# One VectorE instruction fewer per piece of float64 weights, and a new table of costs for the planner, in a fused attention and two-MoE kernel

## The chip, the cores and the metric

One core of one Trainium2 chip runs the whole kernel as one program. The metric is device microseconds of one execution; lower is better. TensorE is called PE here, VectorE DVE, ScalarE ACT, GpSimd POOL, and SP is the engine that issues almost all transfers.

## The reference, cut to what matters

```python
# q, k, v: 4 batches, 8 heads, 576 rows, 64 wide
scores = scale * (q @ k.T)
kth    = the 32nd largest score of each row
attn   = softmax(scores where scores >= kth else -1e9) @ v
x  = attn laid out as [2304, 512]
x2 = ((x @ w_a) * (x @ w_b)) @ w_out      # w_a, w_b 512 x 1536, w_out 1536 x 512, all float64
# second part: 8 experts, each token goes to the expert with the largest logit
logits = x2 @ w_gate
out[token] = gate_w[token] * (relu(x2[token] @ w1[e]) @ w2[e])
```

`w_a`, `w_b` and `w_out` arrive as float64, and no engine computes in float64: the kernel makes float32 of them by handling the two 32-bit words of each number.

## The kernel before, in words

**Weights.** `conv` (L367 to L392) turns one piece of 128 x 512 float64 numbers into float32. There are 36 pieces: 24 of `w_a` and `w_b`, 12 of `w_out`. For one piece SP loads the words (L371); ACT takes the absolute value of the high word with its exponent rescaled (L383); DVE shifts it left by three places and clears the sign (L385); ACT makes the sign, +1 or -1, of the high word (L387); DVE shifts the low word right by 29 and ORs its three top bits in (L388); POOL multiplies by the sign (L391). `split` then cuts the float32 number into a high part (ACT, L396) and a rest (POOL, L397), and both parts are stored in DRAM, in `ws` (L412) for `w_a` and `w_b` and in `wos` (L420) for `w_out`. The pieces use six buffers that belong to later stages (`gT1`, `gH1`, `xh1`, `xl1`, `gT0`, `gH0`), so the traces name them by those.

**Attention.** There are 144 tiles of 128 rows. For a pair of tiles PE makes scores `sp` (L521, or L502 for a tile of leftover rows), ACT copies half of them to `s` (L527), DVE takes the maximum `m` and the minimum `n` of the two halves (L535), and then finds the 32nd largest value with rounds of MAX8 and MATCH_REPLACE8 (L546 to L573). POOL scales the row maximum to `nm` (L549), ACT makes the exponentials `e` (L554), DVE masks and sums them to `am` (L601), PE transposes `am` to `tp` (L627, L609), ACT copies it to `aT` (L631), and PE multiplies by v (L648). `attn_norm` multiplies by the inverse sums: for batches 0 and 1 through an ACT copy and a POOL product (L697, L698), for batches 2 and 3 with one DVE product straight from PSUM (L701).

**First MoE.** `moe1` multiplies by `w_a` and `w_b` (`ab`, L748) and, after the product of both (POOL, L756), by `w_out` (L778). The inner width of 1536 is taken in two halves, each with its own first and second layer. Its weights come from `ws` and `wos` into three buffers `wt`. Batch 0 is done in two groups of rows, 320 and 256, the other batches in one. These matmuls are the filler: PE does them whenever no attention work is ready. `gating` follows each group: logits on PE (L864, L875), some twenty tiny DVE instructions (L883 to L938), a scatter of the rows to `xsort`.

**Second MoE.** Eight experts, after everything else (L1109, L1158); their weights need no conversion from float64.

**What sets the order.** Every step is handed to a planner with its engine, a cost in ns, and a rank `pos`. The planner plays the program through with these costs, takes on each engine the ready step of lowest rank, and the order it finds is the order in which each engine's instructions are then written. An engine works through its instructions strictly in that order. The costs are `c_act`, `c_dve`, `c_ts`, `c_pool`, `c_mm` and a few numbers written at the steps; from one engine to another a fixed delay is added.

## Time and profile before

| | before |
|---|---|
| median of 3 runs | 1207.94 us (1206.33 to 1209.56) |
| the profiled execution, time | 1207.8 us |
| the profiled execution, span | 1206.1 us |
| PE busy | 1082.9 us (90%) |
| DVE busy | 894.5 us (74%) |
| ACT busy | 678.6 us (56%) |
| POOL busy | 462.5 us (38%) |
| mean granted clock of PE | 0.944 |

The span runs from the first to the last instruction of the trace, and the time is 1.7 us more. A busy share is an average over the whole span, while the kernel has stages with different limits, so the shares of single stretches say more.

### The profile page before, as it was taken

To read this page: it belongs to the slowest core of one execution; us is meant where nothing else is said; L and a number is where in the kernel's file an instruction comes from. 1 tells how busy PE (TensorE), PEld (TensorE's weight loads), DVE (VectorE), ACT (ScalarE), POOL (GpSimd) and SP (SyncE) were. 2 spreads that over 40 slices of the span, in tenths; PEclk is the share of its full clock that TensorE was granted. 3 is DMA by queue.
4 is the path that set the end of the run, shared out by engine and by line. 5 is a ranking of instruction groups with operands and counts; after the bars stand their busy time and mean duration, and the time that the engine had idled before them with its cause. 6 is when DMAs were issued, how large, how long until landed. Compare 5 with 4: busy or idle time off the path is not lost.

```text
span 1206.1 us, 21828 instructions
## 1 busy us (share of the span) xinstructions
PE 1082.9 (90%) x7586; PEld 942.3 (78%) x7586; DVE 894.5 (74%) x2636; ACT 678.6 (56%) x1442; POOL 462.5 (38%) x620
## 2 busy tenths in 40 slices
PE   3555696887999999999999999998999999999997
PEld 1333474765788789889888888898998999999996
DVE  6999999999989999999999999920005554544441
ACT  6667676775666666666666655723224454554551
POOL 3555577654445444134646313535134100000001
PEclk9766796987999999999999999999999999999999
DMA  7586577996666423333334242245735555554450
GB/s 260 172 311 200 177 250 252 364 311 205 233 235 208 171 96 114 135 115 120 130 104 137 79 144 78 80 167 206 253 126 177 180 151 191 179 163 148 160 177 21
DMA packets 90476, 210.47 MB, mean 175 GB/s; under 512 B 7363, under 2 KB 44611, under 8 KB 82677
## 3 DMA queue, kind: packets, MB, share of 16 engines
q1 hardware_dynamic: 87141, 199.53, 49.2%
q0 software_dynamic: 3216, 9.46, 2.1%
q8 instruction: 62, 1.02, 0.3%
q14 instruction: 57, 0.47, 0.1%
HBM read 174.31 MB, written 35.25 MB: 174 GB/s over the span
## 4 chain that ended last, share of the span: by engine, by line
PE 53%; DVE 23%; issue 9%; DMA 6%; ACT 4%; POOL 3%; SPq 0%; POOLq 0%; DVEq 0%; ACTq 0%
PE ab L748 18%; PE ab L778 10%; DVE m L559 5%; PE ab L1109 4%; DVE kt L562 4%; DVE am L601 4%; PE pv L648 3%; PE sp L521 3%; PE tp L627 3%; PE ms L1158 2%; PE pv L1158 2%; DMA xsort<-rows,pi 2%; DMA out_dram<-y,ti 2%; DVE m L535 1%; DVE n L535 1%
## 5 line engine op out<-in xcount | busy, mean ns | idle before, releaser
L748 PE MATMUL ab<-xh,wt 128*128 128x320 f32 (+1 forms) x1344 | 302.9, 306 | 3.9 <-ACT sb L733 3.9
L748 PEld LDWEIGHTS ab<-xh,wt 128*128 128x128 f32 x1344 | 226.3, 191 | 17.8 <-issue 11.1
L748 PE MATMUL ab<-xl,wt 128*128 128x320 f32 (+1 forms) x672 | 200.0, 298 | 1.4 <-POOL xl L718 1.4
L559 DVE MATCH_REPLACE8 m<-kt,m 128x288 f32<-128x288 f32 x432 | 188.5, 440 | 0.0
L562 DVE MAX8 kt<-m 128x8 f32<-128x288 f32 x432 | 182.1, 444 | 0.4
L778 PE MATMUL ab<-gH,wt 128*128 128x320 f32 (+1 forms) x768 | 169.4, 304 | 2.9 <-DMA wt<-wos 2.9
L756 POOL TENSOR_TENSOR sa<-sa,sb 128x320 f32<-128x320 f32 (+1 forms) x96 | 82.9, 864 | 154.9 <-ACT sb L733 147.8
L601 DVE SCALAR_TENSOR_TENSOR am<-s,kt,e 128x576 f32<-128x576 f32 x144 | 137.9, 983 | 0.0
L778 PEld LDWEIGHTS ab<-gH,wt 128*128 128x128 f32 x768 | 127.8, 190 | 10.7 <-issue 6.4
L748 PEld LDWEIGHTS ab<-xl,wt 128*128 128x128 f32 x672 | 128.9, 192 | 1.6 <-POOL xl L718 1.6
L554 ACT ACTIVATE e<-s,nm 128x576 f32<-128x576 f32 x144 | 108.9, 781 | 16.8 <-POOL nm L549 15.6
L778 PE MATMUL ab<-gT,wt 128*128 128x320 f32 (+1 forms) x384 | 113.8, 296 | 0.0
L1183 POOL DMA_INDIRECT out_dram<-y,ti x23 | 22.9, 997 | 227.6 <-ACT y L1177 208.7
L1027 DVE TENSOR_TENSOR wp<-raw,wp 128x1024 fp32r<-128x1024 f32 (+1 forms) x73 | 67.4, 943 | 52.8 <-ACT wp L1026 52.6
L527 ACT COPY s<-sp 128x576 f32<-128x576 f32 x128 | 81.9, 640 | 40.5 <-PE sp L521 37.5
L627 PE MATMUL tp<-idr,am 128*128 128x128 f32 x512 | 82.3, 299 | 19.4 <-DVE am L601 16.0
L397 POOL TENSOR_TENSOR gT<-sa,gH 128x320 fp32r<-128x320 f32 (+1 forms) x96 | 83.9, 874 | 40.6 <-ACT gH L396 40.4
L631 ACT COPY aT<-tp 128x512 f32<-128x512 f32 x128 | 71.4, 588 | 41.9 <-PE tp L627 41.6
L627 PEld LDWEIGHTS tp<-idr,am 128*128 128x128 f32 x512 | 63.0, 153 | 37.5 <-DVE am L601 18.9
L521 PE MATMUL sp<-rawk,rawq 64*128 64x288 f32 x128 | 37.6, 666 | 60.3 <-DVE n L534 21.9
L1109 PE MATMUL ab<-xgh,wp 128*128 128x304 f32 (+6 forms) x352 | 89.8, 313 | 1.5 <-DVE gT L1116 0.9
L648 PE MATMUL pv<-aT,vt 128*64 128x320 f32 (+1 forms) x512 | 80.4, 458 | 4.2 <-ACT aT L616 3.4
(280 smaller groups left out, 2409.0 us busy)
## 6 DMA issues: line engine op xcount, KB each, us to landing
wt<-ws SPq DMA_DIRECT2D x54, 1024.0 KB, 5.5
wt<-wos SPq DMA_DIRECT2D x44, 768.0 KB, 4.3
raw<-in_moe_w_dram SPq DMA_DIRECT2D x64, 512.0 KB, 3.8
xsort<-rows SPq DMA_DIRECT2D x8, 771.0 KB, 13.1
wp<-ws SPq DMA_DIRECT2D x6, 1024.0 KB
rawk<-in_kx_dram SPq DMA_DIRECT2D x19, 320.0 KB, 5.7
rawq<-in_qx_dram SPq DMA_DIRECT2D x19, 320.0 KB, 3.7
vt<-in_vx_dram SPq DMA_DIRECT2D x20, 288.0 KB, 2.8
```

The source lines that it names most:

```text
L397: P(POOL, c_pool(cost), pos, lambda: nc.gpsimd.tensor_sub(lo(), src(), fr(hi())), r=rd + wh, w=wl)
L527: P(ACT, c_act(S), pos, lambda hf=hf, sp=sp: nc.scalar.copy(s()[:, :, hf * HS:(hf + 1) * HS], sp()[:, :, 0:HS]), r=[sp], w=[(s, (h, hf)) f ...
L554: P(ACT, c_act(S, True) + 90, pos, lambda h=h, e=e: nc.scalar.activation(e(), s()[:, h], AF.Exp, bias=nm()[:, h], scale=SCALE), r=[(s, (h, ...
L559: P(DVE, c_dve(HS), pos + 5.0 * h, lambda x=x, h=h, j=j: nc.vector.match_replace(out=m()[:, h], in_to_replace=kt(j, 8 * x - 8, 8 * x), in_ ...
L562: P(DVE, c_dve(HS), pos + 5.0 * h, lambda x=x, h=h, j=j: nc.vector.max(out=kt(j, 8 * x, 8 * x + 8), in_=m()[:, h]), r=[(m, h)], w=[KT(j, x)])
L601: P(DVE, c_dve(S) + 60, pos, lambda: nc.vector.scalar_tensor_tensor(am(), sc(), kth(), e(), op0=OP.is_ge, op1=OP.mult, accum_out=r.sum()[: ...
L627: res = nc.tensor.transpose(tp()[:, 512 * h + x * 128:512 * h + (x + 1) * 128], z()[:, 640 * h + x * 128:640 * h + (x + 1) * 128], idf)
L648: nc.tensor.matmul(pv()[64 * h:64 * h + 64, 0:n], u.vt()[:, 256 * h + 64 * j:256 * h + 64 * j + 64], r.aT[h]()[:, j, 0:n], start=(j == 0), ...
L748: res = nc.tensor.matmul(pa()[:, 0:n], view()[:, m, wi, ko, :], xv()[:, ko], start=(ko == 0 and x == 0), stop=(ko == KO - 1 and x == 2))
L756: P(POOL, c_pool(n), pos, lambda: nc.gpsimd.tensor_mul(sa()[:, 0:n], sa()[:, 0:n], sb()[:, 0:n]), r=[sb], w=[sa])
L778: res = nc.tensor.matmul(pa()[:, 0:n], wv()[:, wi, f, :], gv()[:, f, :], start=(f == 0 and x == 0), stop=(f == HB - 1 and x == 2))
L1109: res = nc.tensor.matmul(pa()[:, 0:cap], p1[ko]()[:, wi, f * 128:(f + 1) * 128], xv()[:, ko], start=(ko == 0 and i == 0), stop=(ko == KO - ...
```

## The change: what it does

- **The conversion of a piece.** The DVE instruction at L385 goes. ACT now has three instructions instead of two: the negative numbers with their exponent raised so far that the later shift gives them a sign bit, the top three bits of the low word (from one byte, scaled, with a bias read from a small tile `cut`), and the positive numbers. POOL adds the negative and positive parts, where it multiplied by a sign. DVE has one instruction: shift left by three and OR.
- **Small steps that change engine.** `nm` goes from POOL to ACT (80 instructions); the addition of 1e-9 to the sums goes from POOL to DVE (32); the normalization of batches 2 and 3 goes from one DVE product to an ACT copy and a POOL product (16 of each).
- **The planner's numbers.** `c_act`, `c_ts`, `c_pool`, `c_mm` and the costs of L388, L559 and L601 go up, that of a DVE instruction that reads PSUM goes down a little. DVE steps that follow gating's transposes and its ranking matmuls are planned 10 us and 5 us later than before, except near the end (`lag`).
- The first two pieces' loads are no longer ahead of the first loads of q and k. `SP_` is 0, so that the ranks of the scores are what they were. `G1F` is empty, and what depends on it is as before.

```diff
-                lat = SAME[e] if p.eng == e else LAT[e] + XL.get(p.eng, 0)
+                lat = SAME[e] if p.eng == e else LAT[e] + XL.get(p.eng, 0) + (o.lag if p.eng == "DVE" else 0)
...
 def c_act(n, sbuf=False):
-    return (95 if sbuf else 55) + n * 0.83
+    return (140 if sbuf else 90) + n * 0.83
...
 def c_ts(n):
-    return (n / 2 + 66) / 0.96
+    return (n / 2 + 66) / 0.96 + 200
...
 def c_pool(n):
-    return 150 + n * 2.1
+    return 170 + n * 2.25
...
 def c_mm(n, k=1):
-    return k * (max(n, 256) / 2.4 + 2.5)
+    return k * (max(n, 256) / 2.4 + 13.5)
...
-        if nconv[0] > opts.get("c0", 2):
+        if nconv[0] > opts.get("c0", 0):
             o.deps.add(U[0].mark)
...
-        P(ACT, c_act(CW, True), pos, lambda: nc.scalar.activation(f(), hi(), AF.Abs, scale=2.0 ** -111),
+        P(ACT, c_act(CW, True), pos, lambda: nc.scalar.activation(f(), hi(), AF.Relu, scale=-2.0 ** -79),
           r=[(zr, "r")], w=[(zf, fk)])
-        P(DVE, c_ts(CW), pos, lambda: nc.vector.tensor_scalar(
-            fi(), fi(), 3, 0x7fffffff, op0=OP.logical_shift_left, op1=OP.bitwise_and), w=[(zf, fk)])
-        P(ACT, c_act(CW, True), pos, lambda: nc.scalar.activation(hi(), hi(), AF.Sign), w=[(zr, "r")])
-        P(DVE, c_dve(CW), pos, lambda: nc.vector.scalar_tensor_tensor(
-            fi(), words(0), 29, fi(), op0=OP.logical_shift_right, op1=OP.bitwise_or),
+        P(ACT, c_act(CW, True), pos, lambda: nc.scalar.activation(
+            words(0), top(), AF.Relu, scale=2.0 ** -5, bias=cut),
+          w=[(zr, "r")])
+        P(ACT, c_act(CW, True), pos, lambda: nc.scalar.activation(hi(), hi(), AF.Relu, scale=2.0 ** -111), w=[(zr, "r")])
+        P(POOL, c_pool(CW), pos, lambda: nc.gpsimd.tensor_add(f(), f(), hi()), r=[(zr, "r")], w=[(zf, fk)])
+        P(DVE, c_dve(CW) + 170, pos, lambda: nc.vector.scalar_tensor_tensor(
+            fi(), fi(), 3, words(0), op0=OP.logical_shift_left, op1=OP.bitwise_or),
           r=[(zr, "r")], w=[(zf, fk)], label=f"cv{nconv[0]}")
-        P(POOL, c_pool(CW), pos, lambda: nc.gpsimd.tensor_mul(f(), f(), hi()), r=[(zr, "r")], w=[(zf, fk)])
...
-        P(POOL, 180, pos - 5, lambda: nc.gpsimd.tensor_scalar(
-            nm()[:, 0:nh], r.kt()[:, j0:j0 + nh, 0:1], -SCALE, None, op0=OP.mult),
+        P(ACT, 190, pos - 5, lambda: nc.scalar.activation(
+            nm()[:, 0:nh], r.kt()[:, j0:j0 + nh, 0:1], AF.Copy, scale=-SCALE),
...
-            P(DVE, c_dve(S) + 60, pos, lambda: nc.vector.scalar_tensor_tensor(
+            P(DVE, c_dve(S) + 310, pos, lambda: nc.vector.scalar_tensor_tensor(
...
-        return b in opts.get("pn", (0, 1))
+        return b in opts.get("pn", (0, 1, 2, 3))
...
-        P(POOL, 180, pos - 20, lambda: nc.gpsimd.tensor_scalar(r.sum()[:, 0:nt], r.sum()[:, 0:nt], 1e-9, None, op0=OP.add),
+        P(DVE, 70, pos - 20, lambda: nc.vector.tensor_scalar(r.sum()[:, 0:nt], r.sum()[:, 0:nt], 1e-9, None, op0=OP.add),
...
-            P(PE, 110 * len(GT[g]), pos, lgtr, r=[lg], w=[pl], act=0)
+            P(PE, 110 * len(GT[g]), pos, lgtr, r=[lg], w=[pl], act=0, lag=0 if end or spare else 10000)
...
-        P(PE, 700, pos, rank, r=[K(5)] + [K((7, t + 1)) for t in range(ca, cz) if nt > 2], w=[pr])
+        P(PE, 700, pos, rank, r=[K(5)] + [K((7, t + 1)) for t in range(ca, cz) if nt > 2], w=[pr], lag=0 if end or spare else 5000)
```

The lines of the changed kernel are numbered 2 to 11 higher than those of the kernel before: L532 is the old L521, L538 the old L527, L546 the old L535, L560 the old L549, L565 the old L554, L612 the old L601, L638 the old L627, L759 the old L748 and L789 the old L778; L393, L395, L398, L399 and L400 are the new conversion.

Three places in the orders. The first is the start of DVE's queue, after two set-up instructions; `gT_135` and `gH_137` are the buffers of the first two pieces. Before:

```order
L385 TENSOR_SCALAR gT_135<-gT_135 128x512
L388 SCALAR_TENSOR_TENSOR gT_135<-gT_135 128x512
L385 TENSOR_SCALAR gH_137<-gH_137 128x512
L388 SCALAR_TENSOR_TENSOR gH_137<-gH_137 128x512
L535 TENSOR_TENSOR m<-sp,s 128x576
L535 TENSOR_TENSOR n<-sp,s 128x576
```

In the changed kernel, from the same place to the first mask (rows of the search in between left out):

```order
L546 TENSOR_TENSOR m<-sp,s 128x576
L546 TENSOR_TENSOR n<-sp,s 128x576
L557 MAX kt<-m 128x8 x2
...
L584 MAX kt<-kt 128x8
L400 SCALAR_TENSOR_TENSOR gT_149<-gT_149 128x512
L612 SCALAR_TENSOR_TENSOR am,sum<-s,kt,e 128x576
```

The first piece's DVE work has moved behind the search of the first pair of tiles, and is one instruction. Over the whole order the 36th and last conversion on DVE stands behind 43 of the 144 masks (L601) before, and behind 41 (L612) now.

The second place is ACT's queue at its start, from the first conversion to the first copy of the second pair; `gT_135` and `gT_149` are the first piece's buffer. Before:

```order
L383 ACTIVATE gT_135<-gT_135 128x512
L527 COPY s<-sp 128x2x288
L387 ACTIVATE gT_135<-gT_135 128x512
L383 ACTIVATE gH_137<-gH_137 128x512
L387 ACTIVATE gH_137<-gH_137 128x512
L527 COPY s<-sp 128x2x288
L396 CAST gT_135<-gT_135 128x512
```

And now:

```order
L538 COPY s<-sp 128x2x288 x2
L393 ACTIVATE gT_149<-gT_149 128x512
L560 ACTIVATE nm<-kt 128x2
L395 ACTIVATE gT_149<-gT_149,cut 128x512
L565 ACTIVATE e<-s,nm 128x576 x2
L398 ACTIVATE gT_149<-gT_149 128x512
L538 COPY s<-sp 128x2x288
```

ACT has a third instruction per piece and the scaling `nm`, and the piece no longer stands ahead of the first copies of scores.

The third place is on PE, where the second half of the second layer of batch 0's first group begins (the first L778 or L789 that reads the last six pieces of `w_out`); ahead of it stands attention of batch 1. `pv<-aT` with 256 columns is the product with v of the last unit of batch 0. Before:

```order
L627 MATMUL tp<-idr,am 128x128 x8
L636 MATMUL pv<-idr,am 128x128
L502 MATMUL sp<-kH,qH 128x288 x2
L502 MATMUL sp<-kH,qL 128x288 x2
L502 MATMUL sp<-kL,qH 128x288 x2
L648 MATMUL pv<-aT_2600,vt 64x256
...
L652 MATMUL pv<-aTt,vt 64x256 x2
L627 MATMUL tp<-idr,am 128x128 x8
L690 MATMUL pv<-idr,rr_101 128x128 x2
L778 MATMUL ab<-gH_1335,wt 128x320
```

And now:

```order
L638 MATMUL tp<-idr,am 128x128 x4
L532 MATMUL sp<-kH,qH 128x288 x2
L532 MATMUL sp<-kH,qL 128x288 x2
L532 MATMUL sp<-kL,qH 128x288 x2
L638 MATMUL tp<-idr,am 128x128 x4
L647 MATMUL pv<-idr,am 128x128
L789 MATMUL ab<-gH_1329,wt 128x320
L789 MATMUL ab<-gT_1336,wt 128x320
```

The second layer now starts one pair of tiles earlier, ahead of the product with v and of the pair's transposes. Counted over the order, 390 matmuls of the two layers (L748, L778) stand ahead of the transposes of the 48th tile before, and 420 now; at the 108th tile it is 1698 and 1692. The number of matmuls in all is the same.

## Rows read from the trace of the kernel before

**Rows 1.** The page's busy tenths in 40 slices; PEclk: granted clock.

```profile
PE   3555696887999999999999999998999999999997
DVE  6999999999989999999999999920005554544441
PEclk9766796987999999999999999999999999999999
DMA  7586577996666423333334242245735555554450
```

**Rows 2.** Stretches: length, busy PE PEld DVE ACT POOL, clock, DMA share, GB/s.

```profile
0.00:286.00 286.00, 188.69 (x1008) 134.45 (x1010) 274.09 (x798) 189.16 (x379) 164.82 (x197) 0.80 0.78 258
286.00:786.00 500.00, 491.37 (x3771) 421.49 (x3768) 474.49 (x1543) 315.07 (x713) 213.96 (x312) 0.99 0.39 136
786.00:1197.20 411.20, 402.80 (x2811) 386.37 (x2809) 144.61 (x292) 173.26 (x351) 80.81 (x108) 0.99 0.50 166
```

**Rows 3.** Waits of PE: who waited for whom, total us, times, longest.

```profile
PE sp L521 <- DVE n L534: 21.9, 3, 7.9
PE tp L627 <- DVE am L601: 16.0, 18, 5.0
...
PE ab L778 <- DMA wt<-wos: 2.9, 2, 2.7
```

**Rows 4.** PE's and SP's timelines around 272 to 291 us, with waits in brackets.

```profile
274.54 4.33 SPq L766 DMA_DIRECT2D wt<-wos  x3
...
280.72 1.11 PE L627 MATMUL tp<-idr,am 128*128 128x128 f32 x4 [5.01 <-DVE am L601]
...
290.96 0.39 PE L778 MATMUL ab<-gH,wt 128*128 128x320 f32 x1
291.19 0.31 PE L778 MATMUL ab<-gT,wt 128*128 128x320 f32 x1
291.34 0.46 PE L778 MATMUL ab<-gH,wt 128*128 128x320 f32 x2
```

**Rows 5.** DVE groups, first 290 us: count, busy us, mean ns, idle before.

```profile
L601 DVE SCALAR_TENSOR_TENSOR am<-s,kt,e 128x576 f32<-128x576 f32 x47 | 46.0, 998 | 0.0
...
L385 DVE TENSOR_SCALAR gT<-gT 128x512 int32<-128x512 int32 x11 | 7.2, 655 | 6.2 <-ACT gT L383 6.2
L385 DVE TENSOR_SCALAR x<-x 128x512 int32<-128x512 int32 x14 | 6.6, 474 | 0.0
L385 DVE TENSOR_SCALAR gH<-gH 128x512 int32<-128x512 int32 x11 | 6.3, 574 | 1.2 <-ACT gH L383 1.2
```

**Rows 6.** DVE's timeline near the last piece: start us, length us, instruction.

```profile
262.30 0.68 DVE L388 SCALAR_TENSOR_TENSOR gT<-gT 128x512 int32<-128x512 int32 x1
262.90 0.42 DVE L385 TENSOR_SCALAR gH<-gH 128x512 int32<-128x512 int32 x1
263.24 1.85 DVE L601 SCALAR_TENSOR_TENSOR am<-s,kt,e 128x576 f32<-128x576 f32 x1
```

**Rows 7.** Waits of DVE, columns as in rows 3.

```profile
DVE gb L883 <- PE ms L875: 13.2, 3, 7.1
```

**Rows 8.** Normalization groups: DVE in the span, POOL in the first 290 us.

```profile
L701 DVE TENSOR_TENSOR xf<-xc,pv 128x320 f32<-128x320 f32 (+1 forms) x16 | 7.2, 448 | 12.3 <-PE pv L690 11.2 <-PE pv L692 1.1
...
L698 POOL TENSOR_TENSOR xf<-xc,rs 128x320 f32<-128x320 f32 x5 | 4.3, 861 | 0.0
```

**Rows 9.** ACT groups in the first 290 us, columns as in rows 5.

```profile
L387 ACT ACTIVATE gH<-gH 128x512 f32<-128x512 f32 x11 | 7.5, 680 | 0.2
...
L682 ACT COPY rr<-sum 64x64 f32<-64x64 f32 x10 | 2.4, 240 | 0.1
```

**Rows 10.** Busy time in two stretches, columns as in rows 2.

```profile
210.00:240.00 30.00, 26.85 (x192) 23.08 (x190) 30.00 (x87) 22.21 (x45) 19.00 (x19) 1.00 1.02 368
240.00:270.00 30.00, 24.07 (x162) 19.71 (x163) 29.86 (x90) 22.93 (x51) 16.96 (x18) 0.89 0.94 311
```

**Rows 11.** One line's durations in the span: ns min/median/max, first and last start.

```profile
L601 DVE SCALAR_TENSOR_TENSOR am<-s,kt,e x144: 789/809/2052, 22.0 to 786.8; 128x576 f32<-128x576 f32 x144
```

More of the change, by code (lines that the diff above doesn't have):

```diff
@@ L14 @@
 U32 = mybir.dt.uint32
+U8 = mybir.dt.uint8
 AF = mybir.ActivationFunctionType
@@ L45 @@
 class Op:
-    __slots__ = ("eng", "cost", "fn", "deps", "pos", "n", "outs", "ready", "left", "start", "end", "label", "ins", "act")
+    __slots__ = ("eng", "cost", "fn", "deps", "pos", "n", "outs", "ready", "left", "start", "end", "label", "ins", "act", "lag")
 LAT = {"PE": 210, "ACT": 190, "DVE": 200, "POOL": 130, "SP": 100}
@@ L73, in fixed, with op @@
         return z
-    def op(self, eng, cost, pos, fn, w=(), r=(), label=None, act=1.0):
+    def op(self, eng, cost, pos, fn, w=(), r=(), label=None, act=1.0, lag=0):
         o = Op()
-        o.act = act
+        o.act, o.lag = act, lag
         o.eng, o.cost, o.fn, o.pos, o.n, o.label = eng, cost, fn, pos, len(self.ops), label
@@ L231, in fused_kernel @@
     HALVES = opts.get("halves", (0,))
+    G1F = opts.get("g1f", ())
+    SP_ = opts.get("spp", 0)
     FU = opts.get("fu", range(8))
@@ L310, in fused_kernel @@
         nc.gpsimd.memset(rr_t[i], 0.0)
+    cut = cst.tile([128, 1], F32, name="cut")
+    nc.gpsimd.memset(cut, -0.5 + 2.0 ** -7)
     id2 = cst.tile([128, 64], F32, name="id2")
@@ L558, in attn_tiles @@
             for h, (i, j, kind, _, c) in enumerate(lst):
-                P(DVE, c_dve(HS), pos + 5.0 * h, lambda x=x, h=h, j=j: nc.vector.match_replace(
+                P(DVE, c_dve(HS) + 60, pos + 5.0 * h, lambda x=x, h=h, j=j: nc.vector.match_replace(
                     out=m()[:, h], in_to_replace=kt(j, 8 * x - 8, 8 * x), in_values=m()[:, h], imm_value=NEG),
@@ L810, in moe1 @@
                     marks.append(P_.ops[-1])
-                    if b == 0 and groups == (0,) and hf == 1 and not opts.get("fo", 0):
+                    if b == 0 and groups == ((1,) if 0 in G1F else (0,)) and hf == 1 and not opts.get("fo", 0):
                         for x in range(fi * E // HB, (fi + 1) * E // HB):
@@ L1236, in fused_kernel @@
     for b in range(B):
-        sets = [(g,) for g in (0, 1)] if b in HALVES else [(0, 1)]
+        sets = [(g,) for g in ((1, 0) if b in G1F else (0, 1))] if b in HALVES else [(0, 1)]
         for groups in sets:
```

22 lines of the change are left out of this document (13 added, 9 removed).

## Prediction, made before the changed kernel ran

> **What bounds the kernel now.** I read the profile from the whole to the piece: the busy tenths by slice, busy time in stretches, the waits of the engine that is the bound, and last the timeline at the place where the bound changes hands. In [rows 1] DVE is at nine tenths from 30 us to 780 us (but for one slice at eight) and PE only from about 300 us on; before that PE stands mostly at 5 to 8 tenths, and its granted clock moves between 0.6 and 1.0. The stretches of [rows 2] put numbers on this. Up to 286 us DVE is busy for 274 of 286 us and PE for 189, with 97 us idle. From 286 to 786 us PE is busy for 491 of 500 us and DVE for 474, and from 786 to 1197 us PE is busy for 403 of 411. So there are two bounds: DVE in the first 286 us, PE afterwards.
>
> The waits of PE [rows 3] say the same: the longest totals are for DVE's `n` (21.9 us) and `am` (16.0 us), while a transfer costs PE 2.9 us in all. The hand-over can be watched in [rows 4]: PE waits 5.01 us for `am`, starts its transposes at 280.72 us, and from the first L778 at 290.96 us it has filler in hand. The transfer that brings `wt` for this L778 is issued at 274.54 us.
>
> From this follows how the time is to be worked out. After the hand-over PE has a fixed amount of work, the number of matmuls being the same in both kernels. Whatever brings the hand-over forward, with the same PE work done by then, comes off the time in full. DVE work taken out after it gives nothing as long as DVE has slack there: 500 less 474 is 26 us.
>
> **The change, part by part.** The sum is made against the profiled execution's 1207.8 us, which is the median of the runs (1207.94) within 0.2.
>
> *The removed L385.* All 36 lie ahead of the hand-over. Their busy time is 7.2 + 6.6 + 6.3 = 20.1 us [rows 5]. Neighbours on DVE overlap: in [rows 6] the L388 at 262.30 lasts 0.68 us and the next instruction starts 0.60 us later; the L385 at 262.90 lasts 0.42 and occupies 0.34. So 0.08 us of each is no gain: 20.1 - 36 x 0.08 = 17.2 us. The L388 that stays does shift and OR on the same 128x512 words, so I cost the new one as the old. The 10 additions to the sums that come to DVE ahead of the hand-over (counted over the order) work on five numbers per partition; I give them 0.08 us each, the size of the overlap, which is 0.8 us. No row of before shows them; from nothing to the 0.34 us of an L385 each would be 0 to 3.4 us. Net: **-16.4 us**.
>
> *The order on PE.* At the 48th tile 420 filler matmuls stand ahead where 390 did. These 30 are done while PE would wait. In [rows 4] the matmul at 291.34 starts 0.15 us after the one at 291.19, so 30 of them are 4.5 us of filler that PE need not do after the hand-over: **-4.5 us**, with 0 as the other bound, if the weights aren't there in time. For that I look at what has to come first. The last conversion on DVE stands behind the 41st mask, four to five tiles ahead of the transposes in front of the early L789; before, the last L388 stood behind the 43rd. Of the 291 us up to the first L778, 36 x (0.60 + 0.34) = 34 us go to the conversions [rows 6]; the rest over 48 tiles is about 5 us a tile, so there are some 20 us. Before, the path from the last conversion (right behind the L601 that ends at 265.1 us) to the issue of `wt` (274.54) took 9 us, and the transfer has to land as well. It fits, without much to spare. The planner's new costs act only through such places; after the hand-over the fillers counted at the 108th tile differ by six matmuls, under 1 us, so I cost the rest of the order at nothing.
>
> *Gating planned later on DVE.* DVE waits 13.2 us in three waits for gating's transposes [rows 7]. They lie after the hand-over, where DVE has 26 us of slack, so only what they hold up on PE counts; PE is idle for 500 - 491 = 9 us in this whole stretch. I take **-2 us**, with 0 and -9 as bounds.
>
> *Normalization of batches 2 and 3.* DVE is rid of 16 products of 0.45 us and POOL gets 16 of about 0.86 us [rows 8], ACT 16 copies. All after the hand-over and covered by PE's filler: 0. If that cover were gone, each of the eight chains would be 0.9 us longer.
>
> *ACT's third instruction and `nm`.* L387 takes 0.68 us [rows 9], so 36 more are 24.5 us; of the 80 `nm`, 27 lie ahead of the 48th tile (counted likewise), at the 0.24 us of an L682 [rows 9], 6.5 us. ACT's 189 us become 220 in a stretch of some 267, from 66% to 82%. A fuller queue that works strictly in order is late more often. DVE's own waits in the stretch are 286 - 274 = 12 us at present, 7.4 of them ahead of the first two L385 [rows 5]. I add **+4 us** of new waits; bounds 0 and what the rival below makes of it.
>
> *Transfers.* From 210 to 270 us the DMA share is 1.02 and 0.94 at 368 and 311 GB/s [rows 10]. The same bytes now have to pass in a shorter stretch. DVE's part of these 60 us loses seven or eight of the 36 L385, 3.5 us; I give half of it back: **+2 us**, bounds 0 and 8.
>
> Sum: 1207.8 - 16.4 - 4.5 - 2 + 4 + 2 = 1190.9, so **1191 us**, 1.4% faster.
>
> **The rivals.** *ACT becomes the bound of the first stage: slower.* ACT waits 286 - 189 = 97 us in this stretch now. If these waits were all tied to other producers (scores from PE, `am` from DVE, pieces from POOL) and stayed as long, ACT would need 220 + 97 = 317 us, 31 us more than the stage has, and the kernel would take 1239 us. It decides at waits of 66 us: below, the stage gets shorter. Halfway, with waits of 80 us, the stage takes 300 us and the kernel 1222. Against it: many of the waits are for DVE or for PE that waits for DVE, and these shrink as DVE gets faster. For it: ACT is to do in 0.68 us what DVE did in 0.42, and stands at more than four fifths. The Trainium skill speaks for this rival: its page "ScalarE: Activation LUTs", section "Rules for kernel authors", wants relu, add and mul on VectorE and not on ScalarE; by that rule the change moves work the wrong way, and the rows agree as far as the price of one instruction goes. They don't agree that it matters, since in this stage DVE is full and ACT is not.
>
> *DVE waits for POOL instead: no change.* Before, DVE's two steps had only ACT and the load ahead of them and POOL came after; now L400 needs POOL's addition. A POOL product of 320 columns takes 0.86 us [rows 8], so one of 512 about 1.4 (an estimate from it by columns). If DVE comes to each of the 36 about 0.45 us too early, the 16.4 us are gone and with the waits of the fuller ACT the time is 1206 us. Against it: the instruction stands far behind the loads in DVE's order, with several tiles between two of them.
>
> *Transfers hold the last quarter.* If the transfers between 210 and 270 us were the true limit there, the savings of that quarter and the early filler (4.5 us) would be lost and the landing of the last `wt` would set the hand-over: 1207.8 - 13 - 2 + 4 = 1197 to 1203, say 1200 us. For it speaks the share in [rows 10]; against it that PE waits only 2.9 us for weights.
>
> *More than the sum.* L601 takes 998 ns on average in the first stage [rows 5], where its median in the whole span is 809 [rows 11]; over 47 of them the difference, 9 us, is time in which something held it up. If POOL's shorter queue (without `nm`) were what held it, half of this and gating's 9 us would bring 1179 us.
>
> **How the numbers follow.** Forecast case 0.54, its own range 1184 to 1198; more than the sum 0.13; transfers 0.13; DVE waits for POOL 0.10; ACT the bound 0.10. A measurement of this kernel can tell about 0.3%, 3.6 us, from no change. Faster is the first three cases and a little of the fourth: 0.82. Within 0.3%: the rest of the fourth, 0.08. Slower: 0.10. The range takes in the first, the transfers, most of DVE waiting for POOL and half of the better case: 1180 to 1207, which leaves out nearly 2 in 10.
>
> **What would show each step right or wrong.** Right: PE's unbroken stretch starts near 268 us instead of 291; DVE is busy nearly all the time until then; each piece shows one DVE instruction of 0.6 to 0.7 us or, in a collision, somewhat more; ACT's busy share up to the hand-over is 80 to 85%; from the hand-over to the end PE's idle time is no more than before (some 17 us up to 1197). Wrong: waits of DVE for POOL at L400, or for ACT's copies of scores, of more than 10 us in the first stage; a wait of PE for `wt` at the early L789; a hand-over near 270 us and yet the same end, which would mean new gaps of PE behind it, where the new costs of the planner also change the order.

## The result and the profile after

The changed kernel is slower: four executions took 1219.56 to 1229.42 us, 1221.4 in the median, against 1207.29 us of the kernel before on the same chips; the ratio is 1.0127, 95% interval 1.0078 to 1.0176. A fifth execution, in a slow state with a mean granted clock of 0.679, took 1448.01 us and is left out. The forecast of 1191 us was on the wrong side, and outside its range. The profiled execution took 1229.42 us, with a span of 1227.7; it is the longest of the four, some 8 us above their median, so a difference read from its trace can be larger than that of the medians.

The busy tenths of the page after, beside [rows 1] (the order of the lines is the same):

```profile
PE   3555797979989799999999999999998999999997
...
DVE  7999999998989999989989889831005554443441
PEclk9966697989999889999999999999999999999998
DMA  7796578995566123333333232245635455554540
```

VectorE is still at eight or nine tenths from the second slice to near 800 us, PE still comes in at its nines near 300 us. Some 100 us later there is a dent that before did not have: PE at 7 in the slice of 399 to 430 us, and the clock at 8 there and in the next. The stretches of [rows 2] in the changed kernel, the last one up to 1217 us:

```profile
0.00:286.00 286.00, 197.74 (x1024) 139.76 (x1026) 272.22 (x770) 211.25 (x440) 160.93 (x162) 0.82 0.79 258
286.00:786.00 500.00, 478.74 (x3635) 412.40 (x3636) 458.73 (x1492) 317.86 (x751) 194.84 (x238) 0.98 0.38 133
786.00:1217.00 431.00, 416.29 (x2915) 395.85 (x2916) 161.70 (x351) 185.08 (x381) 92.61 (x123) 1.00 0.48 162
```

PE's last matmul ends at 1197.2 us before and at 1218.8 now; the last row leaves out the final 18 matmuls (1.83 us). PE's idle time falls by 9.0 us up to 286 us (97.3 to 88.3), grows by 12.7 in the middle (8.6 to 21.3) and by 6.3 at the end (8.4 to 14.7), and PE is busy for 11.7 us more (1082.9 to 1094.6); together these are, within rounding, the 21.6 us between the two ends. So PE has a small gain in the first stage, and it is more than lost behind it.

VectorE got nothing out of the first stage. The 48th mask, read from its timeline, ends at 293.9 us in both kernels. The groups of the first 290 us, first the four of L388 in the kernel before (the mask and L385 are in [rows 5]), then what answers to them after; columns as there:

```profile
L388 DVE SCALAR_TENSOR_TENSOR gT<-gT 128x512 int32<-128x512 int32 x11 | 10.7, 976 | 0.0
L388 DVE SCALAR_TENSOR_TENSOR gH<-gH 128x512 int32<-128x512 int32 x11 | 9.2, 840 | 0.0
...
L388 DVE SCALAR_TENSOR_TENSOR x<-xh,x 128x512 int32<-128x512 int32 x7 | 6.2, 890 | 0.0
L388 DVE SCALAR_TENSOR_TENSOR x<-xl,x 128x512 int32<-128x512 int32 x7 | 4.7, 667 | 0.0
```

```profile
L612 DVE SCALAR_TENSOR_TENSOR am<-s,kt,e 128x576 f32<-128x576 f32 x47 | 53.4, 1159 | 0.0
...
L546 DVE TENSOR_TENSOR m<-sp,s 128x576 f32<-128x576 f32 x22 | 16.4, 745 | 11.2 <-ACT s L538 11.0
...
L400 DVE SCALAR_TENSOR_TENSOR gT<-gT 128x512 int32<-128x512 int32 x11 | 12.1, 1100 | 0.4 <-POOL gT L399 0.4
...
L400 DVE SCALAR_TENSOR_TENSOR gH<-gH 128x512 int32<-128x512 int32 x11 | 9.5, 864 | 0.0
L400 DVE SCALAR_TENSOR_TENSOR x<-x,xl 128x512 int32<-128x512 int32 x7 | 8.2, 1176 | 0.0
...
L400 DVE SCALAR_TENSOR_TENSOR x<-x,xh 128x512 int32<-128x512 int32 x7 | 6.6, 949 | 0.0
...
L682 DVE TENSOR_SCALAR sum<-sum 128x5 f32<-128x5 f32 (+1 forms) x10 | 3.9, 393 | 0.0
```

L385 and its 20.1 us are gone. But the same 47 masks take 7.4 us more (46.0 to 53.4), the instruction that stayed 5.6 us more (30.8 to 36.4), and the ten additions 3.9 us where the sum had 0.8. Of 20.1 us, 3.2 are left, and less when overlaps are counted once: up to the 48th mask VectorE is busy for 280.1 us instead of 282.0. Its idle time there grows from 11.9 to 13.8 us, which uses up the rest. Most of its waits for ACT's copies are not new:

```profile
DVE m L546 <- ACT s L538: 11.0, 5, 7.2
```

The longest, 7.2 us, is the wait for the first copy of scores at the start, where VectorE waited 7.4 us for the first two pieces before. The other four, 3.8 us, compare with 1.1 before.

What lengthens them is seen on the timelines of VectorE and POOL (start us, length us, instruction, wait), first at 106 to 112 us, then at 131 us:

```profile
106.34 1.29 POOL L399 TENSOR_TENSOR gT<-gT 128x512 f32<-128x512 f32 x1 [2.10 <-ACT gT L398]
107.61 1.73 POOL L399 TENSOR_TENSOR gH<-gH 128x512 f32<-128x512 f32 x1
109.30 1.77 POOL L408 TENSOR_TENSOR xl<-x,xl 128x512 fp32r<-128x512 f32 x1
...
106.47 1.72 DVE L400 SCALAR_TENSOR_TENSOR x<-x,xl 128x512 int32<-128x512 int32 x1
108.11 1.83 DVE L612 SCALAR_TENSOR_TENSOR am<-s,kt,e 128x576 f32<-128x576 f32 x1
...
109.88 1.81 DVE L612 SCALAR_TENSOR_TENSOR am<-s,kt,e 128x576 f32<-128x576 f32 x1
...
131.57 0.80 DVE L612 SCALAR_TENSOR_TENSOR am<-s,kt,e 128x576 f32<-128x576 f32 x1
```

The two engines end in turn: POOL at 107.63, VectorE at 108.19, POOL at 109.34, VectorE at 109.94, POOL at 111.07, VectorE at 111.69. Each instruction starts when its engine is free and ends some 0.6 us (VectorE) or 1.2 us (POOL) after the other's last. A mask lasts 1.8 us there, alone 0.80. Going through the 47 masks of each kernel: those beside which POOL does nothing average 0.81 us in both; they are 18 before and 8 after. The others carry all of the excess over 0.81 us, 8.9 us before and 16.5 after.

The dent of PE, as the stretch of 390 to 440 us of the kernel before and of the changed one:

```profile
390.00:440.00 50.00, 45.89 (x342) 37.72 (x342) 48.34 (x165) 31.53 (x70) 23.57 (x35) 0.97 0.39 137
```

```profile
390.00:440.00 50.00, 38.05 (x256) 30.43 (x255) 47.22 (x164) 28.84 (x66) 14.68 (x18) 0.83 0.27 97
```

86 matmuls fewer, and a lower clock. By the end of the 48th mask PE had started 22 more matmuls than before (1078 and 1056 of the records), by the 66th 43 more (1848 and 1805), by the 72nd 2 fewer (1994 and 1996), and by the 90th 29 fewer (2633 and 2662). The lead was used up. By time, the changed kernel ends its 1750th matmul 0.5 us earlier than before (382.8 and 383.2), its 2250th 11.3 us later (464.9 and 453.6), its 4750th 16.0 later, and its last 21.6 later: half of the loss falls into these 500 matmuls. From 400 to 440 us VectorE has no gap (40.0 us busy, 39.1 before) and PE's timeline has the attention's own products and their waits, with no filler between them:

```profile
400.82 0.40 PE L532 MATMUL sp<-kH,qH 64*128 64x288 f32 x2 [1.21 <-DVE n L546]
...
405.76 1.11 PE L620 MATMUL tp<-idr,am 128*128 128x128 f32 x4 [2.48 <-DVE am L612]
...
408.92 4.01 PE L659 MATMUL pv<-aT,vt 128*64 128x320 f32 x16 [1.62 <-ACT aT L627]
```

The second half of the second layer, whose start the prediction watched, begins at 281.33 us, 9.6 us earlier than the first L778 of [rows 4], and PE waits for its weights, as the prediction had feared:

```profile
281.33 0.41 PE L789 MATMUL ab<-gH,wt 128*128 128x320 f32 x1 [2.35 <-DMA wt<-wos]
```

Over the span these waits are 9.4 us in five, four of them before 350 us; before they were 2.9 us in two [rows 3], both after 900 us.

### The profile page after: what moved, and what is told of

It reads as the page before. It is cut to its first block, busy times and chain, and to the rows that moved or that the text cites. A ratio compares the mean times of both kernels' runs of the same rounds, so it can differ in the third digit from the quotient of the medians.

```text
span 1227.7 us, 21766 instructions
## 1 busy us (share of the span) xinstructions
PE 1094.6 (89%) x7586; PEld 949.7 (77%) x7586; DVE 893.9 (73%) x2616; ACT 715.8 (58%) x1574; POOL 451.3 (37%) x525
## 3 DMA queue, kind: packets, MB, share of 16 engines
q8 instruction: 62, 1.02, 0.3%
## 4 chain that ended last, share of the span: by engine, by line
PE 49%; DVE 13%; DMA 13%; issue 11%; ACT 8%; POOL 5%; SPq 1%; POOLq 0%; ACTq 0%; DVEq 0%
PE ab L759 18%; PE ab L789 10%; PE pv L659 3%; PE tp L638 3%; DVE m L570 3%; DMA xsort<-rows,pi 3%; PE ab L1120 3%; PE sp L532 3%; DVE kt L573 3%; DVE am L612 2%; DMA out_dram<-y,ti 2%; PE ms L1169 2%; PE pv L1169 2%; ACT aT L642 1%; DMA raw<-in_moe_w_dram 1%
## 5 line engine op out<-in xcount | busy, mean ns | idle before, releaser
L759 PE MATMUL ab<-xh,wt 128*128 128x320 f32 (+1 forms) x1344 | 304.2, 307 | 0.7 <-DMA wt<-ws 0.7
L759 PEld LDWEIGHTS ab<-xh,wt 128*128 128x128 f32 x1344 | 226.7, 192 | 17.6 <-issue 14.5
L759 PE MATMUL ab<-xl,wt 128*128 128x320 f32 (+1 forms) x672 | 200.4, 298 | 0.2 <-POOL xl L729 0.2
L789 PE MATMUL ab<-gH,wt 128*128 128x320 f32 (+1 forms) x768 | 173.5, 307 | 10.2 <-DMA wt<-wos 9.4
L612 DVE SCALAR_TENSOR_TENSOR am<-s,kt,e 128x576 f32<-128x576 f32 x144 | 147.5, 1053 | 0.0
L789 PEld LDWEIGHTS ab<-gH,wt 128*128 128x128 f32 x768 | 130.0, 192 | 18.6 <-DMA wt<-wos 9.4
L767 POOL TENSOR_TENSOR sa<-sa,sb 128x320 f32<-128x320 f32 (+1 forms) x96 | 80.1, 834 | 166.2 <-ACT sb L744 164.7
L759 PEld LDWEIGHTS ab<-xl,wt 128*128 128x128 f32 x672 | 129.2, 192 | 0.6 <-POOL xl L729 0.5
L789 PE MATMUL ab<-gT,wt 128*128 128x320 f32 (+1 forms) x384 | 114.7, 299 | 0.0
L565 ACT ACTIVATE e<-s,nm 128x576 f32<-128x576 f32 x144 | 108.6, 780 | 0.8
L638 PE MATMUL tp<-idr,am 128*128 128x128 f32 x512 | 86.0, 302 | 18.3 <-DVE am L612 8.1
L538 ACT COPY s<-sp 128x576 f32<-128x576 f32 x128 | 81.8, 639 | 26.8 <-PE sp L532 23.2
L659 PE MATMUL pv<-aT,vt 128*64 128x320 f32 (+1 forms) x512 | 83.2, 469 | 12.7 <-ACT aT L627 9.9
L638 PEld LDWEIGHTS tp<-idr,am 128*128 128x128 f32 x512 | 63.8, 154 | 38.6 <-ACT aT L642 14.8
L744 ACT ACTIVATE sa<-ab 128x320 f32<-128x320 f32 (+1 forms) x120 | 49.3, 411 | 63.7 <-PE ab L759 40.2
```

What stands on the lines that cost most here:

```text
L538: P(ACT, c_act(S), pos - SP_, lambda hf=hf, sp=sp: nc.scalar.copy(s()[:, :, hf * HS:(hf + 1) * HS], sp()[:, :, 0:HS]), r=[sp], w=[(s, (h, ...
L565: P(ACT, c_act(S, True) + 90, pos, lambda h=h, e=e: nc.scalar.activation(e(), s()[:, h], AF.Exp, bias=nm()[:, h], scale=SCALE), r=[(s, (h, ...
L612: P(DVE, c_dve(S) + 310, pos, lambda: nc.vector.scalar_tensor_tensor(am(), sc(), kth(), e(), op0=OP.is_ge, op1=OP.mult, accum_out=r.sum()[ ...
L638: res = nc.tensor.transpose(tp()[:, 512 * h + x * 128:512 * h + (x + 1) * 128], z()[:, 640 * h + x * 128:640 * h + (x + 1) * 128], idf)
L659: nc.tensor.matmul(pv()[64 * h:64 * h + 64, 0:n], u.vt()[:, 256 * h + 64 * j:256 * h + 64 * j + 64], r.aT[h]()[:, j, 0:n], start=(j == 0), ...
L759: res = nc.tensor.matmul(pa()[:, 0:n], view()[:, m, wi, ko, :], xv()[:, ko], start=(ko == 0 and x == 0), stop=(ko == KO - 1 and x == 2))
```

## The experiments

Theory A put the loss on VectorE's first stage (longer instructions, waits for ACT), theory B on the planner's new numbers, theory C on the small moved steps. Ratios are to the kernel before measured beside it, with their 95% intervals; a difference between two runs is clear of noise where these intervals lie apart, and uncertain where they overlap; the ends of masks are read from VectorE's timeline.

**e1, the conversion alone.** On the kernel before, with `cut` and its memset:

```diff
+        P(ACT, ... nc.scalar.activation(f(), hi(), AF.Relu, scale=-2.0 ** -79) ...
+        P(ACT, ... nc.scalar.activation(words(0), top(), AF.Relu, scale=2.0 ** -5, bias=cut) ...
+        P(ACT, ... nc.scalar.activation(hi(), hi(), AF.Relu, scale=2.0 ** -111) ...
+        P(POOL, ... nc.gpsimd.tensor_add(f(), f(), hi()) ...
+        P(DVE, c_dve(CW), ... fi(), fi(), 3, words(0), logical_shift_left, bitwise_or ...
```

> The kernel before with nothing but the new conversion of a piece (three activations, POOL's addition, one VectorE instruction); the planner's numbers and the small steps (nm on POOL, sums on POOL, normalization of batches 2 and 3 on VectorE) are those of before. Theory A, what the removed VectorE instruction gave is eaten in the first stage by VectorE's longer instructions and its waits for ACT: 1204 to 1211 us, 48th mask near 293 us as in both kernels. Theory B, the conversion gains and the planner's new numbers and lags lose it: 1188 to 1197 us, 48th mask at 275 to 283 us. Theory C, the small moved steps lose it: the same 1188 to 1197 us here.

1205.07 us, ratio 0.9998 (0.9979 to 1.0018): no change. The 48th mask ends at 290.2 us, 3.7 earlier. The masks are longer still than in the changed kernel, 41 of 48 lie beside an instruction of POOL:

```profile
L608 DVE SCALAR_TENSOR_TENSOR am<-s,kt,e 128x576 f32<-128x576 f32 x48 | 58.2, 1240 | 0.0
```

VectorE waits 8.3 us for the first scores at its start and not for POOL. So the conversion by itself wins nothing, as theory A has it; but it does not lose either, so what makes the changed kernel slower must come with the other parts.

**n1, L385 left out of the kernel before.**

```diff
-        P(DVE, c_ts(CW), pos, lambda: nc.vector.tensor_scalar(
-            fi(), fi(), 3, 0x7fffffff, op0=OP.logical_shift_left, op1=OP.bitwise_and), w=[(zf, fk)])
+        P(DVE, c_ts(CW), pos, lambda: None, w=[(zf, fk)])
```

> The kernel before, in its own order on every engine, with the 36 VectorE instructions of L385 (shift and mask) left out of the program, so that the converted weights are not the reference's. It gives the price of one VectorE instruction per piece by itself. If the sum of the prediction prices it rightly: 48th mask 17 us earlier, at 277 us, and 1189 to 1193 us. If POOL's work of a piece then lies beside other VectorE instructions (theory A): L601 at 1100 ns and more in the first 290 us instead of 998, 48th mask 3 to 10 us earlier. If time won ahead of the 48th mask is given back behind it: mask 17 us earlier and the end less than 8 us earlier.

1195.94 us, ratio 0.991 (0.9893 to 0.9928): 11 us faster; none of the three expectations fits it whole. The 48th mask ends at 282.1, 11.8 us earlier, and the span is 12.4 us shorter (1193.7). With the order kept, then, time won before the hand-over does come off the end in full, as the prediction had it; it is 11 to 12 us and not 16. The mask got shorter, not longer:

```profile
L600 DVE SCALAR_TENSOR_TENSOR am<-s,kt,e 128x576 f32<-128x576 f32 x49 | 44.9, 936 | 0.5
```

What is missing to 16.4 are waits: 5.8 us for ACT's copies of scores and 3.3 for POOL's additions to the sums in the first 290 us, against 1.1 and 1.0.

**n2, the conversion alone without POOL's two steps.** On e1:

```diff
-        P(POOL, c_pool(CW), pos, lambda: nc.gpsimd.tensor_add(f(), f(), hi()), r=[(zr, "r")], w=[(zf, fk)])
+        P(POOL, c_pool(CW), pos, lambda: None, r=[(zr, "r")], w=[(zf, fk)])
-        P(POOL, c_pool(cost), pos, lambda: nc.gpsimd.tensor_sub(lo(), src(), fr(hi())), r=rd + wh, w=wl)
+        P(POOL, c_pool(cost), pos, (lambda: None) if cost == CW else lambda: nc.gpsimd.tensor_sub(...), ...)
```

> The kernel with the new conversion alone (run e1), in the same order, with POOL's two steps of a piece (the addition and the subtraction of the split) left out of the program, so that the converted weights are not the reference's. Theory A, VectorE's instructions on two inputs in SBUF are lengthened by POOL's: the mask instruction at 800 to 900 ns instead of 1240 in the first 290 us, the one instruction of a piece near 600 ns, 48th mask 15 us and more earlier than in that run (275 us or less), time 1185 to 1195 us. Rival, the long instructions have another cause: mask instruction still above 1100 ns, 48th mask at 285 to 290 us.

1187.04 us, ratio 0.9831 (0.9815 to 0.9848). The 48th mask ends at 271.0, 19.2 us earlier than in e1.

```profile
L609 DVE SCALAR_TENSOR_TENSOR am<-s,kt,e 128x576 f32<-128x576 f32 x52 | 46.2, 917 | 0.1
...
L396 DVE SCALAR_TENSOR_TENSOR gT<-gT 128x512 int32<-128x512 int32 x11 | 8.0, 726 | 0.0
L396 DVE SCALAR_TENSOR_TENSOR gH<-gH 128x512 int32<-128x512 int32 x11 | 7.4, 677 | 0.0
```

The mask falls from 1240 to 917 ns; 26 of 52 now stand beside nothing of POOL, at 0.81 us. The others, at 1.02 us, stand beside POOL's other work (normalization, the products and rests of the first MoE), which is still there. The rival is out: POOL's work lengthened them. The 19.2 us are all that POOL's two steps cost VectorE in e1, not what the change added to it: the kernel before has these two steps too, and wasn't run without them.

**n3, the changed kernel without POOL's two steps.** The same edit on the changed kernel.

> The changed kernel in its own order, with POOL's two steps of a piece (addition and subtraction of the split) left out of the program, so that the converted weights are not the reference's. On the kernel with the conversion alone this took 18 us off (1205 to 1187). If lengthened VectorE instructions cost the changed kernel as much: 1204 to 1209 us, with the mask instruction below 950 ns in the first 290 us and the 48th mask at 277 us. If its loss lies in the order alone: 1217 to 1224 us.

1213.67 us, ratio 1.0065 (1.0045 to 1.0085), in between: some 8 us off the changed kernel's 1221.4 (the two intervals overlap by a little), and still 0.65% above the kernel before, which has those steps. The 48th mask is 12.1 us earlier (281.8).

```profile
L613 DVE SCALAR_TENSOR_TENSOR am<-s,kt,e 128x576 f32<-128x576 f32 x49 | 43.4, 910 | 0.0
...
L683 DVE TENSOR_SCALAR sum<-sum 128x5 f32<-128x5 f32 (+1 forms) x10 | 1.8, 182 | 0.0
```

So both theories have a part: the longer instructions eat the gain, and the order costs besides. The tiny additions fall from 393 to 182 ns: they too were held up by POOL. But up to the 48th mask VectorE's busy time falls by 25.8 us, and only 12.1 come off: 13.7 us come back as waits. VectorE's `m` now waits 23.6 us for copies of scores in the first 290 us, 7.3 of them at the start, where the changed kernel has 11.0 and 7.2. In n2, without the small steps, only 1.1 us came back. So ACT's queue stands right behind POOL as the next thing that VectorE waits for; which of the differences between the two kernels makes it so was not tried.

**e14, the conversion in the order of before.** All else keeps its place; the second and third activation and POOL's addition stand where the sign was taken (`low` issues these three):

```diff
+        P(ACT, c_act(CW, True), pos, lambda: nc.scalar.activation(f(), hi(), AF.Relu, scale=-2.0 ** -79), ...
+        P(DVE, c_ts(CW), pos, lambda: None, w=[(zf, fk)])
+        P(ACT, c_act(CW, True), pos, low, w=[(zr, "r")])
+        P(DVE, c_dve(CW), pos, lambda: nc.vector.scalar_tensor_tensor(fi(), fi(), 3, words(0), ...
+        P(POOL, c_pool(CW), pos, lambda: None, r=[(zr, "r")], w=[(zf, fk)])
```

> The new conversion with every other instruction where it stands in the kernel before on every engine: the first activation stands where the old one did, the other two and POOL's addition where the sign was taken, VectorE's one instruction where L388 stood; nothing stands where L385 and POOL's product stood. If the new conversion lengthens VectorE's other instructions because plan and order around it change (run e1): 1194 to 1200 us, as with L385 left out of the kernel before (1196), faster than both kernels. If it is the conversion's own third activation and POOL's addition ahead of VectorE: 1202 to 1210 us, mask instruction at 1100 ns and more in the first 290 us.

1219.29 us, ratio 1.0096 (1.0079 to 1.0113): slower, beyond both expectations. The 48th mask ends at 306.7, 12.8 us later than before.

```profile
L611 DVE SCALAR_TENSOR_TENSOR am<-s,kt,e 128x576 f32<-128x576 f32 x43 | 47.6, 1124 | 0.5
...
L398 DVE SCALAR_TENSOR_TENSOR gH<-gH 128x512 int32<-128x512 int32 x11 | 10.9, 993 | 2.3 <-POOL gH L393 2.3
...
L398 DVE SCALAR_TENSOR_TENSOR gT<-gT 128x512 int32<-128x512 int32 x11 | 9.1, 826 | 14.3 <-POOL gT L393 14.3
```

Here VectorE waits 16.6 us for POOL's addition, which is what the second rival of the prediction had feared, and the masks are longer as well. Of these, 11.1 us are for the first two pieces, where VectorE waited 7.4 us for ACT before. POOL in its turn waits for the new activations (19.4 us for `gT` in the first 290 us), so the run doesn't part the third activation from the addition. In e1 the planner, which knows of that wait, puts VectorE's instruction later and the waits go; what stays are the lengthened instructions.

**e11, the conversion alone, with the first two pieces started as late as in the changed kernel.**

```diff
-        if nconv[0] > opts.get("c0", 2):
+        if nconv[0] > opts.get("c0", 0):
```

> The kernel with the conversion alone, and the first two pieces started as late as the others, as in the changed kernel (there the 10th mask ends at 70.0 us, here at 75.6). If the 5 us of the start come through to the end: 1198 to 1202 us, faster than both kernels. If the shifted order takes them back: 1203 to 1215 us.

1206.56 us, ratio 0.9997 (0.9984 to 1.001). The 10th mask comes 2.5 us earlier than in e1, the 48th 1.5 later. Nothing is gained. PE is 8.9 us ahead of the kernel before at its 1750th matmul and 0.4 at its 2250th: this run loses its lead in the same stretch as the changed kernel (278 matmuls from 390 to 440 us, clock 0.86), with none of the new numbers, lags or small steps. No version with the whole computation is faster than the kernel before by more than its interval.

**e3, the planner's new numbers on the kernel before.** All costs and lags of the diff, no instruction changed.

> The kernel before with the planner's new numbers and lags and nothing else; every instruction is that of before. Theory A: 1205 to 1212 us. Theory B: 1216 to 1230 us, with PE's idle time after 286 us at 30 us and more instead of 17. Theory C: 1205 to 1212 us.

1233.68 us, ratio 1.0228 (1.0203 to 1.0252). The numbers alone cost 27 us there: the 48th mask is 8.7 us later, and PE's idle time from 286 us to its last matmul is 33.7 us instead of 17.0. Theory B, for this kernel, and somewhat beyond its range.

**e5, the lags alone on the kernel before.**

```diff
-            P(PE, 110 * len(GT[g]), pos, lgtr, r=[lg], w=[pl], act=0)
+            P(PE, 110 * len(GT[g]), pos, lgtr, r=[lg], w=[pl], act=0, lag=0 if end or spare else 10000)
...
+        P(PE, 700, pos, rank, r=..., w=[pr], lag=0 if end or spare else 5000)
```

> The kernel before with nothing but the lags of gating's transposes and ranks in the plan. If the lags are what makes the new plan slow: 1220 to 1232 us, as with all the new numbers. If the costs are: 1204 to 1210 us.

1223.37 us, ratio 1.0125 (1.0101 to 1.0149). The 48th mask ends at 293.9 as before, so all of it is lost behind the hand-over:

```profile
286.00:786.00 500.00, 479.16 (x3646) 408.39 (x3644) 470.87 (x1512) 307.93 (x691) 204.72 (x297) 0.99 0.37 132
```

PE is idle for 20.8 us there instead of 8.6. In the stretch of 390 to 440 us it runs 308 matmuls instead of 342, a smaller dent than that of the changed kernel (256).

**e6, VectorE's new costs alone on the kernel before.** The additions of 60, 170, 200 and 310 ns and the lower cost on PSUM.

> The kernel before with VectorE's new costs alone in the plan (60, 170, 200 and 310 ns more, 21 ns less on PSUM). If VectorE's tiles, priced longer, put scores behind too much filler: 1218 to 1230 us and over 35 us of VectorE's waits from 290 to 790 us where before has 24. If another of the numbers does it: 1204 to 1212 us.

1250.9 us, ratio 1.0366 (1.0348 to 1.0384), more than all numbers together and beyond both expectations. VectorE's `m` waits 22.7 us for copies of scores from 290 to 790 us (10.3 before) and its reciprocals of the sums 15.8 for POOL's additions (3.9 before), and the 144th mask ends 54.7 us later (842.9). The other numbers of the diff take part of this back.

**e2, the changed kernel with the plan of before.** All costs and lags as they were.

> The changed kernel with every number of the planner as before (costs of ACT, VectorE, POOL and TensorE, the additions of 60, 170 and 310 ns, no lag). Theory A: the loss is not in the plan, 1215 to 1226 us as the changed kernel. Theory B: 1190 to 1202 us. Theory C: 1215 to 1226 us.

1223.38 us, ratio 1.0159 (1.0114 to 1.0204). Theory B fails here: on the changed instructions the old numbers are no better than the new. Against e1, which differs by the small steps and the start of the first pieces alone, the small steps cost some 18 us (e11 shows the start to be worth nothing).

**e10, the changed kernel without the lags.** The edit of e5 taken back.

> The changed kernel without the lags of gating's transposes and ranks. If a lag costs as much here as on the kernel before (1223 against 1207 us): 1205 to 1212 us, with the 48th mask where it was (294 us). If the order is slow for other reasons too: 1216 to 1228 us.

1217.53 us, ratio 1.0087 (1.0065 to 1.0108): within the second expectation. That is 4 us below the changed kernel, but the two intervals overlap, so a cost of the lags isn't shown here; the 16 us that they cost on the kernel before are outside of it. The dent is there without the lags: 251 matmuls from 390 to 440 us, at a clock of 0.83.

**e4, the changed kernel with the small steps as before.** `nm` and the addition to the sums on POOL, `pn` at (0, 1).

> The changed kernel with the small steps as before (nm and the addition to the sums on POOL, normalization of batches 2 and 3 on VectorE); conversion and planner's numbers stay changed. Theory A: 1215 to 1226 us, VectorE's instructions as long as in the changed kernel. Theory B: 1215 to 1226 us. Theory C: 1195 to 1208 us, with fewer than 15 us of waits of VectorE for ACT's copies of scores where the changed kernel has 35.

1217.64 us, ratio 1.01 (1.0072 to 1.0128). Against 1.0127 (1.0078 to 1.0176) the small steps cost little or nothing under the new numbers, where they cost 1.6% under the old. Beside e3 this run shows the new conversion, with the later start of its first pieces, to be worth 1.3% under the new numbers (1.0228 to 1.01), where it is worth nothing under the old.

**e7, e8, e9, one small step each on e1**: `nm` on ACT, the addition on VectorE, normalization of batches 2 and 3 on POOL and ACT.

> The kernel with the new conversion alone (run e1, 1205 us) and nm on ACT besides; plan as before. The conversion with all the small steps (run e2) took 1223 us, so the small steps cost 18 us together there. If nm is what costs: 1215 to 1223 us, with 10 us and more of VectorE's waits for ACT's copies of scores in the first 290 us. If not: 1200 to 1209 us.

> The kernel with the new conversion alone and the additions to the sums on VectorE besides; plan as before. If these additions are what costs (0.39 us each instead of 0.08): 1210 to 1218 us. If not: 1200 to 1209 us.

> The kernel with the new conversion alone and the normalization of batches 2 and 3 on POOL and ACT besides; plan as before. If it costs what the sum of the prediction says, nothing: 1202 to 1208 us. If it lengthens the end of the attention or the work behind the last mask (run e2 had 425 us behind the last mask, run e1 414): 1210 to 1220 us.

1213.97, 1216.95 and 1210.62 us; ratios 1.0056 (1.0037 to 1.0075), 1.0076 (1.0052 to 1.01) and 1.0023 (1.0009 to 1.0037). Together they are 1.6%, what e2 has over e1. Each is above the kernel before; that of e9 is not clear of e1's interval. e7 lies between its two expectations, e8 and e9 within those by which the step costs. `nm` costs without the 10 us of waits that were expected of it: in the first 290 us `m` waits 2.0 us for copies of scores (3.7 in e1) and `n` 4.2 (1.5). Still its 48th mask comes 6.4 us later than in e1, and its 144th 6.7 later, so most of the loss falls into the first stage: 2.0 us are longer masks, 3.6 us more idle time of VectorE. From 290 to 790 us `m` waits 14.0 us (5.5 in e1), which by the 144th mask has cost next to nothing.

**e13, the addition on VectorE with every other instruction in place.** On e1:

```diff
-        P(POOL, 180, pos - 20, lambda: nc.gpsimd.tensor_scalar(r.sum()[:, 0:nt], r.sum()[:, 0:nt], 1e-9, ...
+        P(POOL, 180, pos - 20, lambda: nc.vector.tensor_scalar(r.sum()[:, 0:nt], r.sum()[:, 0:nt], 1e-9, ...
```

> The kernel with the conversion alone, with the 32 additions to the sums run on VectorE but planned as POOL's, so that every other instruction keeps its place on every engine. With the plan made for VectorE (run e8) it took 1217 us, without the move 1205. If the additions themselves cost (32 of 0.37 us): 1213 to 1218 us. If what costs is that the plan moves other instructions when an addition changes engine: 1203 to 1208 us.

1209.89 us, ratio 1.0027 (1.0015 to 1.0039), in between. The durations of the 32 additions, and those of e8:

```profile
L678 DVE TENSOR_SCALAR sum<-sum x32: 141/158/1522, 47.2 to 793.0; 128x5 f32<-128x5 f32 x16, 128x4 f32<-128x4 f32 x16
```

```profile
L678 DVE TENSOR_SCALAR sum<-sum x32: 146/316/1034, 45.9 to 801.5; 128x5 f32<-128x5 f32 x16, 128x4 f32<-128x4 f32 x16
```

(Least, median and greatest length in ns.) By the ratios the additions themselves cost 0.3%, some 3.5 us (its interval and e1's overlap by a little), and the places that the plan then gives to others 0.5%, some 6 us more.

## Why the prediction was wrong

- **The removed L385, 16.4 us: the size was wrong, and it is the step that failed first.** Alone and in a fixed order the removal is worth 11 to 12 us (n1), because waits for ACT and POOL grow. In the changed kernel it is worth nothing at the 48th mask, because the sum costed "the new one as the old" and left all other VectorE instructions at their lengths: the one that stayed takes 5.6 us more, the masks 7.4. That POOL's steps lengthen them is shown by n2 and n3: without these the same masks fall from 1240 to 917 and from 1159 to 910 ns, and the 48th mask comes 19 and 12 us earlier. The prediction had seen that 9 us of L601 were a hold-up, and in its rival "more than the sum" had it shrink; it grew from 998 to 1159 ns.
- **The order of PE, -4.5 us, and the rest of the order at nothing: wrong, and the largest term.** The 48th mask ends at the same time in both kernels, and PE's last matmul 21.6 us later. The early filler, for which the sum had -4.5 us, was there (22 matmuls more at the 48th mask), after a wait for `wt` of 2.35 us; it was used up between the 66th and the 72nd mask, with PE idle and its clock down from 0.97 to 0.83 in 390 to 440 us. Of the 11.7 us more of PE's busy time some 3.7 come from there, an estimate: 256 matmuls took 38.05 us, and at the 134 ns of the row of before, whose mix of matmuls is another, they would take 34.4. Where the others come from is not settled. That a plan alone can do this is shown on the kernel before, where its numbers move the time by 1.3 to 3.7% (e5, e3, e6); on the changed instructions the old numbers are no better (e2).
- **The new conversion needs POOL ahead of VectorE.** Kept in the old order, VectorE waits 16.6 us for it (e14); with the order moved, it hardly waits, and more masks lie beside POOL's work (41 of 48 in e1 and 39 of 47 in the changed kernel, instead of 29 of 47). Either way the gain of n1 is gone. The rival "VectorE waits for POOL" was right that POOL takes the gain and wrong about the form: in the changed kernel these waits are 0.4 us. (Its 1206 us is about 1 short of its own terms, 1190.9 + 36 x 0.45.)
- **Time before the hand-over comes off in full: right** in a fixed order (n1: 11.8 us at the mask, 11 to 12 at the end; n2 against e1: 19.2 at the mask, 18 between the medians).
- **Gating later, -2 us: not borne out.** The three waits of [rows 7] stand at 803, 807 and 906 us, behind the last mask (788.2) and so outside the stretch of 286 to 786 us from which the 26 and 9 us were taken. In the changed kernel the same three are longer, 27.9 us in all where they were 13.2. The lags cost 16 us on the kernel before (e5); on the changed one a cost is not clear of noise (e10). That on the kernel before they move gating's filler away from the stretch of 390 to 440 us is argued from the counts of matmuls there, and not shown by itself; in the changed kernel the dent doesn't need them (e10).
- **The additions to the sums, 0.8 us: too small.** 3.9 us in the first stage, some 3.5 us for the whole move with everything else in place (e13).
- **Normalization at nothing: nearly right**, 0.25% (e9).
- **ACT's fuller queue, +4 us: not too small in the first stage.** Of the 11.0 us of waits for copies of scores 7.2 stand at the start, in place of 7.4 us of before; all of VectorE's idle time up to the 48th mask grew by 1.9 us. ACT is no bound of this stage: it is busy 211 of 286 us. But n3 shows that its copies are what VectorE waits for next, and `nm` alone costs 0.6% (e7).
- **Transfers, +2 us**: the DMA share in the first stage is 0.79 beside 0.78 in [rows 2], but PE now waits 6.9 us for `wt` before 290 us, where it waited for none. What this costs in the end wasn't tried by itself.

By the old plan first, the loss is 0 for the conversion, 1.6% for the small steps and nothing for the new numbers (e1, e2, the changed kernel); by the numbers first, it is +2.3%, then -1.3% for the conversion and +0.3% for the small steps (e3, e4, the changed kernel); the last step of either is within the noise. The parts don't add up to one account, since each of them moves the order of the others. What stays open is why the changed kernel's order runs out of filler near 400 us, and why a given set of numbers makes a good order; the runs show only that the order before is a good one for the instructions before.

## What to carry to other kernels

Before a VectorE instruction is priced at what it takes in the trace, look whether the long ones lie beside POOL's: if they do, the lengths of its neighbours belong to the price. Leaving one out did not lengthen them here (n1: masks at 936 ns instead of 998); the new order of the conversion, with POOL's addition ahead of VectorE's instruction, did (e1: 1240). Where a planner sets the order, an edit is two edits, and a run in which one instruction is left out or moved with all others in place tells them apart. Work that PE does earlier than it must was no gain here, since a later stretch then had nothing else to fill PE's waits (the changed kernel, e11).

## What the runs showed of the hardware

A VectorE instruction that reads two tensors in SBUF takes about twice as long beside POOL's addition or subtraction of 512 columns: the mask 1.8 us instead of 0.81. POOL's own instruction grew too, from 1.29 us where it came first to 1.73 and 1.77 where VectorE did. An instruction with one of its two inputs in PSUM was untouched: in the first 290 us the maximum of scores in PSUM and in SBUF (L546) took 745 ns after, where its counterpart L535 took 740 before, and 746 in n2 without POOL's steps. The Trainium skill says in "SBUF — State Buffer", section "SBUF: two separate sides", that VectorE with two SBUF inputs and GpSimd hold a shared pair of ports in turn for a whole instruction; the trace agrees, with the ends in turn from 107.63 to 111.69 us. A tensor-scalar addition on five numbers per partition is held up in the same way: 141 ns at the least, up to 1522 in e13, and 182 on average in n3 where POOL's steps were gone, against 393 in the changed kernel.
